# Key maxima spread one u product earlier, the subtractions on VectorE, and ten of sixteen channel weight rows split inside the second phase

## The chip, the cores and the metric

The kernel runs on one core of a Trainium2 chip. The metric is the device time of one execution in microseconds (us). The engines are named as in the profile: PE is TensorE, DVE is VectorE, ACT is ScalarE, POOL is GpSimd, and SP is the engine that issues most of the DMAs.

## What is computed

For each of 8 samples (576 tokens, 8 heads of 64) a linear attention feeds a gated block, and that feeds a channel block:

```
q_s = softmax(q, over head_dim); k_s = softmax(k, over the 576 tokens)
x   = q_s @ (k_s^T @ v)                       # 576 x 512 per sample
u, v = split(gelu(x @ w_in)); v_n = layernorm(v) * g_ln
x   = x + (u * (w_sg @ v_n + b_sg)) @ w_out
u   = x + token_mix(x; U, V)                  # rank 32
out = u + relu(u @ w_ch1) @ w_ch2             # 512 -> 2048 -> 512
```

The weights w_in, w_out, U, V, w_ch1 and w_ch2 are float64 in memory and are turned into pairs of float32 parts (a high and a low one) on the chip. A product of two such pairs is made with three matmuls: high by high, high by low, low by high.

## The kernel before

**Two phases.** The first phase loops over the samples, b = 0 to 7. In each it makes the v products (`emit_Vh`, tile pv, five token tiles t), the u products (`emit_Uh`, pu, four feature tiles f), the token products (`emit_S`, pS, four) and the output products (`emit_y`, py, four). The token mix of the sample before (`emit_yT`, `emit_U`, `emit_PV`; tiles pt, pp, pw) is woven into the v products, and the attention of the next sample into the rest. The second phase is the channel block: 9 blocks of 512 tokens, and in each 16 rows fc of channel weights. A step is `ch2` of one row (tile acc, 12 matmuls) and `ch1` of the row three further (tile ph, 12 matmuls). ACT writes the high part hh (L670), DVE the low part hl (L671).

**Who orders the work.** PE runs in program order throughout. In samples 1 to 6 DVE runs in program order too, and ACT, POOL and SP are ordered by the framework's planner. In sample 0, and from sample 7 to the end of the kernel, ACT runs in program order instead and DVE is ordered by the planner. PSUM products of the first phase share three buffers (`ps2`): a product has to wait until DVE or ACT has read the one three before it.

**The attention of the next sample.** `k_fold` takes the key maximum over token tiles, `k_max` transposes it on PE (pm), reduces it on DVE and builds two diagonal matrices on POOL; `k_spread` turns them into a broadcast on PE (pb), which ACT copies into kmx. `k_sub` subtracts it from five key tiles: tiles 0 and 1 on POOL, tiles 2 to 4 on DVE (all five on POOL for sample 1). `q_max` and `q_sub` do the same for queries per head, `q_total` sums the exponentials (DVE), `q_norm` multiplies by the reciprocal (all five on POOL).

**The pieces.** `Conv` converts one 128 x 256 piece of a float64 weight: a DMA brings the words into a buffer `stg`, a clamp (L163) makes the high word safe, ACT takes it to a float (L164), DVE shifts it (L170) and merges the low bits in (L171), ACT copies the high part and POOL subtracts to get the low part. `more(n)` takes n pieces one stage on; the tuples in `mid` and `spread` say how many are taken at each token tile t, each f and each output tile. A row of channel weights is four pieces. All 16 rows are converted in the first phase, with their clamp on DVE, and stored to `wd` in device memory; `load_w` reads them back through POOL's queue before the second phase uses them.

Of the kernel before, what the change touches and what calls it, by code (L numbers as in the profile page):

```python
# [8 lines left out]
F32 = mybir.dt.float32  # L9
F32R = mybir.dt.float32r  # L10
U32 = mybir.dt.uint32
# [11 lines left out]
def fused_kernel(tc, q, k, v, w_in, g_ln, w_sgT, b_sg, w_out, U, V, w_ch1, w_ch2, outT):  # L23
# [13 lines left out]
    LINE = 128  # L37
    VLEN = -(-(NT + 1) * NC * VW * 4 // LINE) * LINE // 4
    NFC = w_ch1.shape[0]
    BLK = 512  # L40
    NBLK = B * S // BLK
    TR = [P] * NT + [R]
# [6 lines left out]
    def tt(eng, out, a, b, op):  # L49
        return eng.tensor_tensor(out=out, in0=a, in1=b, op=op)  # L50
# [12 lines left out]
        return cm.__enter__(), lambda: cm.__exit__(None, None, None)  # L63

    dram, close_dram = opened("dram", space=bass.MemoryType.DRAM)
    wd = dram.tile([NFC, 2, P, 2, C], F32, name="wd")
    u2d = dram.tile([NC, P, B * S], F32, name="u2d")
    ps2, close_ps2 = opened("ps2", 3, space=PSUM)
    ps1, close_ps1 = opened("ps1", 2, space=PSUM)
# [18 lines left out]
    pool.memset(ones32, 1.0)  # L88
    ones = cst.tile([P, P], F32R, name="ones")
    pool.tensor_copy(ones, ones32)  # L90
    cpow = cst.tile([P, 2], F32, name="cpow")
    pool.memset(cpow[:, 0:1], 1e-6)
    pool.memset(cpow[:, 1:2], -0.5)

    qt = att.tile([P, NT + 1, C], F32, name="qt")
    gl = cst.tile([P, 24], F32, name="gl")[:, 0:NF]
# [44 lines left out]


    CW = 256

    def split_w(hi, lo, s, eng):
        copy(hi, s)
# [2 lines left out]
    def stage():  # L149
        return stgp.tile([P, S], F32, tag="stg", name="stg", bufs=5)  # L150

    def words(n):

        return stage().bitcast(U32)[:, 0 : 2 * n].rearrange("p (n j) -> p n j", j=2)

    def pairs(src):
        return src.bitcast(U32).rearrange("p (n j) -> p n j", j=2)

    def exponent(w, n, eng):

        t = stgp.tile([P, HS], F32, tag="f32", name="f32")[:, 0:n]
        hi = as_f32(w[:, :, 1])
        eng.tensor_scalar(out=hi, in0=hi, scalar1=F64_MOST, scalar2=-F64_MOST, op0=ALU.min, op1=ALU.max)  # L163
        act.activation(t, hi, AF.Prelu, scale=F64_SCALE, alpha=F64_SIGN)  # L164
        return t
# [109 lines left out]
            cols = slice(h * HS, (h + 1) * HS)  # L275
            yield ConvV(V[:, cols], lambda o=v_w[:, cols]: o, eng)

    def conv_ch(eng):

        for fc in range(NFC):  # L280
            for i, src in enumerate((w_ch1, w_ch2)):
                for c in range(0, C, CW):

                    def outs(fc=fc, i=i, cols=slice(c, c + CW)):
                        hl = stgp.tile([P, 2, CW], F32R, tag="chw", name="chw")
                        return hl[:, 0], hl[:, 1], lambda: sp.dma_start(wd[fc, i, :, :, cols], as_f32(hl))

                    piece = Conv(src[fc, :, c : c + CW], outs, eng)
                    piece.clamp = dve
                    yield piece  # L290
# [43 lines left out]
        km = kx_t[b] = tmpp.tile([P, S], F32, tag="gt", name="kmx")[:, 0:C]  # L334
        copy(km, pb.rearrange("p c e -> p (c e)"))

    def k_sub(b, t, eng=None):
        kt, n = k_t[b], TR[t]
        tt(eng if eng else pool if t < 2 or b == 1 else dve, kt[0:n, t], kt[0:n, t], kx_t[b][0:n], ALU.subtract)

    def k_exp(b):
        kt = k_t[b]
# [11 lines left out]
        dve.tensor_reduce(out=q_s[b][0 : TR[t], t], in_=q3(t), op=ALU.max, axis=mybir.AxisListType.X)  # L354

    def q_sub(b, t, eng=dve):
        eng = pool if b == 1 else eng
        n = TR[t]
        tt(eng, q3(t), q3(t), q_s[b][0:n, t].unsqueeze(2).to_broadcast([n, H, D]), ALU.subtract)

# [140 lines left out]
    def stats(b, t):  # L501
        ge, n = ln[b, t], TR[t]
        bst = tmpp.tile([P, 6], F32, tag="bst", name="bst", bufs=3)
        mv = tmpp.tile([P, 2], F32, tag="mv", name="mv", bufs=3)
        dve.bn_stats(out=bst[0:n], in_=ge[0:n])
        dve.bn_aggr(out=mv[0:n], in_=bst[0:n])
        tt(dve if b == 0 else pool, mv[0:n, 1:2], mv[0:n, 1:2], cpow[0:n, 0:1], ALU.add)
        last[pool] = tt(pool, mv[0:n, 1:2], mv[0:n, 1:2], cpow[0:n, 1:2], ALU.pow)
        ln[b, t] = (ge, mv)

    def emit_ln(b, t):
        ge, mv = ln.pop((b, t))
        n = TR[t]
        shift = tmpp.tile([P, 1], F32, tag="sh", name="sh", bufs=2)
        dve.scalar_tensor_tensor(
            out=shift[0:n], in0=mv[0:n, 0:1], scalar=-1.0, in1=mv[0:n, 1:2], op0=ALU.mult, op1=ALU.mult
        )
        act.activation(ge[0:n], ge[0:n], AF.Identity, bias=shift[0:n], scale=mv[0:n, 1:2])
        h = wrk.tile([P, F], F32R, tag=f"vh{t}", name=f"vh{t}")
        if t < NT:  # L520
            l = wrk.tile([P, F], F32R, tag=f"vl{t}", name=f"vl{t}")
            copy(h, ge)
            low(pool, l, ge, h)
            vh[b, t] = (h, l)
        else:
            copy(h[0:R], ge[0:R])
            low(dve, h[64 : 64 + R], ge[0:R], h[0:R])
            vh[b, t] = h
# [107 lines left out]
    def load_w(pl, fc):  # L636
        for i in range(2):
            hl = pl.tile([P, 2, C], F32R, tag=f"w{i}_{fc}", name=f"w{i}_{fc}", bufs=1)
            pool.dma_start(hl, wd[fc, i])
            w12[i, fc] = (hl[:, 0], hl[:, 1])  # L640

    blk = {}
# [77 lines left out]
            yield  # L720


    mid = ((0, 0, 0, 0, 0), (1, 1, 1, 1), (1, 1, 0, 0), (0, 1, 1, 1))
    spread = [mid] * B
    spread[0] = ((2, 2, 2, 2, 1), (2, 2, 2, 2), (1, 1, 1, 1), (1, 1, 1, 1))
    spread[B - 1] = ((0, 0, 0, 0, 1), (1, 1, 1, 1), (1, 1, 1, 0), (1, 1, 1, 1))
    order = {0: (act,), B - 1: (act,)}
    load_k(0)
    load_q(0)
    load_v(0)  # L730
# [8 lines left out]
    pieces.extend(conv_w_out(0, pool))  # L739
    pieces.extend(conv_w_out(CW, pool))  # L740
    pieces.extend(conv_uv(pool))
    pieces.extend(conv_ch(pool))
    with in_order(dve):
        run(k_fold(0))
        q_max(0, 0)
# [30 lines left out]
    for b in range(B):  # L776
# [11 lines left out]
        for t in range(NT + 1):  # L788
            emit_Vh(b, t)
            if nxt:  # L790
                if t == 0:
                    with behind(dve):
                        if b == 0:
                            q_max(nxt, 0)
                            q_max(nxt, 1)
                        q_max(nxt, 2)
                elif t == 1:
                    with behind(dve):
                        q_max(nxt, 3)
                        q_max(nxt, 4)  # L800
                elif t in (2, 3):
                    with behind(dve):
                        next(fold)
                        next(fold)
            if t < NT:
                stats(b, t)
            more(spread[b][0][t])
            if t > 0:
                emit_ln(b, t - 1)
            if t == NT:  # L810
                stats(b, t)
            if b > 0:
                for t2 in {0: (2,), 1: (3, 4)}.get(t, ()):
                    emit_yT(b - 1, t2)
            if t == 2 and b > 0:
                for t2 in range(NT + 1):
                    emit_U(b - 1, t2)
            if t in (3, 4) and b > 0:
                for c in range(2 * t - 6, 2 * t - 4):
                    emit_PV(b - 1, c)  # L820
# [1 line left out]
        if nxt:  # L822
            k_max(nxt)
        for f in range(NF):
            if nxt and f == 3:
                k_spread(nxt)
            if b == 0:
                more(spread[b][1][f])
            emit_Uh(b, f)
            if f == 0:  # L830
                emit_ln(b, NT)
                if nxt:
                    load_v(nxt)
            if nxt:
                with behind(pool):
                    if f == 0:
                        q_sub(nxt, 0)
                    elif f == 1:
                        q_sub(nxt, 1)
                        q_sub(nxt, 2)  # L840
                    elif f == 2:
                        q_sub(nxt, 3)
                        q_sub(nxt, 4)
                    elif f == 3:
                        for t in range(NT + 1):
                            k_sub(nxt, t)
            if b > 0:
                more(spread[b][1][f])
            if not nxt and f == 1:
                load_w(p2a, 0)  # L850
                split_u(p2a, 0)
        if nxt:
            for t in range(NT + 1):
                q_exp(nxt, t)
            k_exp(nxt)
            q_total(nxt)
            for t in range(NT + 1):
                q_norm(nxt, t)

        for f in range(NF):  # L860
            emit_S(b, f)
# [20 lines left out]
        for c in range(NC):  # L882
            more(spread[b][3][c])
            emit_y(b, c)
            if nxt and 0 < c < 3:
                emit_qT(nxt, 1 + c)
                if c == 2 and b + 2 < B:
                    load_q(b + 2)
        if b + 2 < B:
            q_max(b + 2, 0)  # L890
            q_max(b + 2, 1)
        if nxt:
            emit_xT(nxt, 0)
            emit_xT(nxt, 1)
# [27 lines left out]
    acc_p, close_acc = opened("acc_p", space=PSUM)  # L922
    p2w, close_p2w = opened("p2w", side="left")
    b_p, close_bp = opened("b_p", side="left")
    steps = [(n, fc) for n in range(NBLK) for fc in range(NFC)]
    for fc in range(3, NFC):
        load_w(p2w, fc)
    for i, (n, fc) in enumerate(steps):
        if fc == 2 and n + 1 < NBLK:
            load_u((p2a, b_p)[(n + 1) % 2], n + 1)  # L930
        if fc == 8 and n + 1 < NBLK:
            split_u((p2a, b_p)[(n + 1) % 2], n + 1)
        ch2(n, fc)
        if i + 3 < len(steps):
            n2, fc2 = steps[i + 3]
            ch1(n2, fc2, h_p.tile([P, BLK], F32, tag="ph", name="ph"), p2b)
    part.__exit__(None, None, None)
    for close in (close_bp, close_p2w, close_acc, close_hp, close_p2b, close_p2a, close_edge, close_dram):
        close()


# [38 lines left out]
```

## Time and profile before

| what | value |
|---|---|
| median of 3 runs | 1484.12 us (1480.53 to 1484.29) |
| profiled execution | 1485.02 us, span 1483.2 us |
| mean granted TensorE clock | 0.975 of full speed |
| PE busy | 1393.7 us, 94% of the span |
| DVE busy | 644.5 us, 43% |
| ACT busy | 481.4 us, 32% |
| POOL busy | 388.4 us, 26% |

Busy time counts each instruction from its start to its end. Matmuls overlap, so a busy PE is not one at its peak. An idle PE shows in the timeline as a bracket behind an instruction: how long PE had been idle before it, and whose work it was waiting for.

### The profile page before, as it was taken

Reading aid. Unit: us, or ns where it says so; the run is one execution under the profiler, and the core shown is the slowest. Engines: PE = TensorE matmul, PEld = TensorE weight load, DVE = VectorE, ACT = ScalarE, POOL = GpSimd, SP = SyncE. Lnnn points to the kernel's source line nnn. Section 1 sums busy time; section 2 is a strip of 40 time slices with the busy share of each in tenths; the row PEclk is TensorE's granted clock in tenths of the full one; section 3 lists DMA queues with packets and bytes.
Section 4 is the critical chain, followed back from the end, with each engine's and each line's share of the span. In section 5 each row is a group of like instructions: output and inputs, shape, how many; then the busy total and the mean of one; then the engine's idle time right before and its main releaser. Section 6 shows DMA issues by size and latency. Waiting matters only on the chain.

```text
span 1483.2 us, 19165 instructions
## 1 busy us (share of the span) xinstructions
PE 1393.7 (94%) x7672; PEld 1197.6 (81%) x7672; DVE 644.5 (43%) x1073; ACT 481.4 (32%) x842; POOL 388.4 (26%) x460
## 2 busy tenths in 40 slices
PE   4777989899989999999999999999999999999998
PEld 3666888888888888888888888888888888888887
DVE  7787777878777787755111111111111111111111
ACT  4554746465565656452011111111110111111110
POOL 6783443545353534541310101001010000101000
PEclk9998999999999999999999999999999999999999
DMA  6624234242524252343901010010101001010000
GB/s 175 186 78 133 87 123 121 87 149 85 154 95 146 97 160 83 111 142 107 370 0 57 1 57 1 20 38 0 57 1 57 0 8 50 0 57 1 29 0 29
DMA packets 80313, 117.01 MB, mean 79 GB/s; under 512 B 6496, under 2 KB 41312, under 8 KB 80224
## 3 DMA queue, kind: packets, MB, share of 16 engines
q1 hardware_dynamic: 75616, 99.02, 21.4%
q0 software_dynamic: 4608, 16.78, 3.3%
q8 instruction: 60, 0.98, 0.3%
q14 instruction: 29, 0.24, 0.0%
HBM read 80.12 MB, written 35.65 MB: 78 GB/s over the span
## 4 chain that ended last, share of the span: by engine, by line
PE 57%; DVE 1%; DMA 1%; issue 1%; ACT 0%; POOL 0%; DVEq 0%; ACTq 0%; SPq 0%; POOLq 0%
PE ph L47 26%; PE acc L47 26%; PE py L47 2%; PE pS L47 1%; PE pu L47 1%; PE pv L47 1%; DMA w<-wd 0%; DMA stg<-in_w_ch_dram 0%; PE pp L47 0%; DVE gl L50 0%; PE pt L594 0%; DVE gt L560 0%; DVE yl L50 0%; DVE xl L50 0%; POOL gt L50 0%
## 5 line engine op out<-in xcount | busy, mean ns | idle before, releaser
L47 PE MATMUL ph<-uh,w 128*128 128x512 f32 x1152 | 378.3, 389 | 0.1
L47 PE MATMUL acc<-hh,w 128*128 128x512 f32 x1152 | 377.7, 389 | 0.0
L671 DVE SCALAR_TENSOR_TENSOR hl<-ph,hh 128x512 fp32r<-128x512 f32 x144 | 99.5, 691 | 615.1 <-ACT hh L670 615.1
L670 ACT ACTIVATE hh<-ph 128x512 fp32r<-128x512 f32 x144 | 86.1, 598 | 685.2 <-PE ph L47 685.2
L47 PEld LDWEIGHTS acc<-hh,w 128*128 128x128 f32 x1152 | 216.4, 188 | 45.1
L47 PEld LDWEIGHTS ph<-uh,w 128*128 128x128 f32 x1152 | 216.1, 188 | 45.3 <-DMA w<-wd 0.5
L47 PE MATMUL ph<-ul,w 128*128 128x512 f32 x576 | 224.1, 389 | 0.0
L47 PE MATMUL acc<-hl,w 128*128 128x512 f32 x576 | 224.1, 389 | 0.0
L50 POOL TENSOR_TENSOR ul<-u,uh 128x512 fp32r<-128x512 f32 x32 | 40.3, 1295 | 590.5 <-ACT uh L56 590.5
L47 PEld LDWEIGHTS ph<-ul,w 128*128 128x128 f32 x576 | 108.2, 188 | 22.4
L47 PEld LDWEIGHTS acc<-hl,w 128*128 128x128 f32 x576 | 108.0, 188 | 22.2
L50 POOL TENSOR_TENSOR chw<-f,chw 128x256 fp32r<-128x256 f32 x64 | 55.7, 876 | 122.7 <-ACT chw L56 69.4
L47 PE MATMUL py<-gh,wo_h 128*128 128x288 f32 x256 | 63.2, 332 | 11.5 <-DVE gt L560 11.5
L47 PE MATMUL pS<-sg_h,vh 128*128 128x288 f32 x256 | 56.4, 302 | 15.2 <-DVE gt L560 9.3
L47 PE MATMUL pu<-xh,wi_h 128*128 128x288 f32 x256 | 58.9, 313 | 9.6 <-ACT ge L495 4.3
L47 PE MATMUL py<-gl,wo_h 128*128 128x288 f32 x256 | 60.3, 320 | 0.0
L47 PE MATMUL py<-gh,wo_l 128*128 128x288 f32 x256 | 59.4, 316 | 0.0
L47 PE MATMUL pu<-xl,wi_h 128*128 128x288 f32 x256 | 58.0, 310 | 0.0
L170 DVE TENSOR_SCALAR f<-f 128x256 uint32<-128x256 uint32 (+2 forms) x91 | 48.5, 533 | 21.7 <-ACT f L164 21.5
L47 PE MATMUL pu<-xh,wi_l 128*128 128x288 f32 x256 | 57.9, 309 | 0.0
L171 DVE SCALAR_TENSOR_TENSOR f<-stg,f 128x256 uint32<-128x256 uint32 (+2 forms) x91 | 56.0, 615 | 2.7
L47 PEld LDWEIGHTS py<-gh,wo_h 128*128 128x128 f32 x256 | 46.2, 213 | 13.5 <-issue 12.5
(146 smaller groups left out, 2282.6 us busy)
## 6 DMA issues: line engine op xcount, KB each, us to landing
stg<-in_w_ch_dram SPq DMA_DIRECT2D x64, 256.0 KB, 2.7
wd<-chw SPq DMA_DIRECT2D x64, 256.0 KB, 2.5
w<-wd POOLq DMA_DIRECT2D x32, 512.0 KB, 9.8
u2d<-yt SPq DMA_DIRECT2D x32, 288.0 KB, 2.1
u<-u2d SPq DMA_DIRECT2D x9, 1024.0 KB, 6.4
out_dram<-res SPq DMA_DIRECT2D x36, 256.0 KB, 2.1
vt<-in_v_dram SPq DMA_DIRECT2D x32, 256.0 KB, 6.9
qt<-in_q_dram SPq DMA_DIRECT2D x7, 1024.0 KB, 6.0
```

The costliest lines, as they stand in the source:

```text
L47: pe.matmul(out, lhsT, rhs, start=first, stop=last)
L50: return eng.tensor_tensor(out=out, in0=a, in1=b, op=op)
L170: dve.tensor_scalar(out=b, in0=b, scalar1=3, scalar2=None, op0=ALU.logical_shift_left)
L171: dve.scalar_tensor_tensor(out=b, in0=w[:, :, 0], scalar=29, in1=b, op0=ALU.logical_shift_right, op1=ALU.bitwise_or)
L670: act.activation(a, ph, AF.Relu)
L671: dve.scalar_tensor_tensor(out=l, in0=ph, scalar=0.0, in1=as_f32(a), op0=ALU.max, op1=ALU.subtract)
```

## The change

The edit has five parts. (1) Rows 0 to 5 of the channel weights are still converted in the first phase and go through device memory; rows 6 to 15 (40 pieces) are converted while the second phase runs, four pieces a step, straight into their weight tiles, with buffers of their own. Samples 1 to 6 now convert two pieces each, where they converted nine. (2) `k_spread` stands before the third u product instead of the fourth. (3) `k_sub` and `q_sub` run on DVE for every sample but sample 0's own queries, and the first two tiles of `q_norm` move from POOL to DVE. (4) The epsilon of the variance is added on DVE instead of POOL. (5) All five `q_max` of a sample stand at token tiles 0 to 2; sample 0 has DVE in program order and ACT ordered by the planner.

```diff
+    EARLY = 6
-    wd = dram.tile([NFC, 2, P, 2, C], F32, name="wd")
+    wd = dram.tile([EARLY, 2, P, 2, C], F32, name="wd")
...
-        return stage().bitcast(U32)[:, 0 : 2 * n].rearrange("p (n j) -> p n j", j=2)
+        if pools["stg"] is stgp:
+            s = stage()
+        else:
+            s = pools["stg"].tile([P, 2 * CW], F32, tag="stg", name="stg", bufs=4)
+        return s.bitcast(U32)[:, 0 : 2 * n].rearrange("p (n j) -> p n j", j=2)
...
                     def outs(fc=fc, i=i, cols=slice(c, c + CW)):
+                        if fc >= EARLY:
+                            h, l = w12[i, fc]
+                            return h[:, cols], l[:, cols]
...
-    def k_sub(b, t, eng=None):
+    def k_sub(b, t, eng=dve):
         kt, n = k_t[b], TR[t]
-        tt(eng if eng else pool if t < 2 or b == 1 else dve, kt[0:n, t], kt[0:n, t], kx_t[b][0:n], ALU.subtract)
+        tt(eng, kt[0:n, t], kt[0:n, t], kx_t[b][0:n], ALU.subtract)
...
     def q_sub(b, t, eng=dve):
-        eng = pool if b == 1 else eng
...
-        tt(dve if b == 0 else pool, mv[0:n, 1:2], mv[0:n, 1:2], cpow[0:n, 0:1], ALU.add)
-        last[pool] = tt(pool, mv[0:n, 1:2], mv[0:n, 1:2], cpow[0:n, 1:2], ALU.pow)
+        dve.tensor_scalar(out=mv[0:n, 1:2], in0=mv[0:n, 1:2], scalar1=1e-6, scalar2=None, op0=ALU.add)
+        tt(pool, mv[0:n, 1:2], mv[0:n, 1:2], half[0:n], ALU.pow)
...
-            pool.dma_start(hl, wd[fc, i])
+            if fc < EARLY:
+                pool.dma_start(hl, wd[fc, i])
...
-    mid = ((0, 0, 0, 0, 0), (1, 1, 1, 1), (1, 1, 0, 0), (0, 1, 1, 1))
+    mid = ((0, 0, 0, 0, 0), (0, 0, 0, 0), (0, 0, 0, 0), (0, 1, 1, 0))
-    spread[0] = ((2, 2, 2, 2, 1), (2, 2, 2, 2), (1, 1, 1, 1), (1, 1, 1, 1))
+    spread[0] = ((2, 2, 2, 1, 0), (2, 1, 1, 1), (3, 2, 2, 1), (1, 1, 1, 1))
-    order = {0: (act,), B - 1: (act,)}
+    order = {B - 1: (act,)}
...
-            if nxt and f == 3:
+            if nxt and f == 2:
                 k_spread(nxt)
...
+                for t in ((0, 1), (2, 3, 4), (), ())[f]:
+                    q_sub(nxt, t)
+                for t in ((), (), (0, 1), (2, 3, 4))[f]:
+                    k_sub(nxt, t)
...
-                q_norm(nxt, t)
+                q_norm(nxt, t, dve if t < 2 else pool)
...
+    pools["stg"], close_words = opened("words", side="left")
+    pieces.extend(conv_ch(range(EARLY, NFC), pool))
...
         ch2(n, fc)
+        more(4)
```

## Rows read from the trace of the kernel before

**Rows 1.** Windows: us, then busy PE, PEld, DVE, ACT, POOL, granted clock, DMA.

```profile
40.00:138.60 98.60, 73.05 (x480) 65.31 (x479) 76.33 (x120) 48.03 (x99) 63.80 (x76) 0.86 0.43 124
138.60:220.00 81.40, 75.38 (x528) 68.48 (x527) 61.92 (x107) 46.25 (x79) 36.34 (x42) 0.94 0.36 111
220.00:300.00 80.00, 73.45 (x535) 66.84 (x533) 61.86 (x107) 46.85 (x80) 36.19 (x42) 0.98 0.39 121
...
542.00:623.60 81.60, 75.84 (x532) 69.02 (x531) 63.11 (x112) 46.83 (x80) 36.42 (x42) 0.94 0.36 112
...
703.10:1483.20 780.10, 775.71 (x3422) 641.64 (x3420) 120.91 (x180) 100.95 (x173) 53.53 (x57) 1.00 0.12 40
```

**Rows 2.** Waits of PE over the span: total us, times, longest us.

```profile
PE py L47 <- DVE gt L560: 11.5, 7, 8.2
PE pt L429 <- DVE gt L560: 11.0, 6, 1.8
...
PE pS L47 <- DVE gt L560: 9.3, 6, 1.7
PE pw L47 <- DVE yt L50: 6.8, 7, 1.0
```

**Rows 3.** Windows of 10 us behind the pt wait, in two samples.

```profile
279.00:289.00 10.00, 7.64 (x45) 7.37 (x46) 9.57 (x19) 4.32 (x8) 2.78 (x3) 0.83 0.17 53
...
441.00:451.00 10.00, 7.91 (x37) 7.43 (x38) 9.40 (x18) 4.33 (x8) 2.77 (x3) 0.66 0.16 54
```

**Rows 4.** Timeline of DVE, 421 to 433 us: start, duration, instruction.

```profile
421.79 4.63 DVE L50 TENSOR_TENSOR kt<-kt,kmx 128x512 f32<-128x512 f32 x3
...
431.64 0.76 DVE L560 SCALAR_TENSOR_TENSOR gt<-pS,gl,bb 128x576 f32<-128x576 f32 x1
```

**Rows 5.** Timeline of POOL, 409 to 437 us.

```profile
409.68 1.04 POOL L50 TENSOR_TENSOR diag<-ident,ml 128x512 fp32r<-128x512 f32 x1
...
421.64 3.08 POOL L50 TENSOR_TENSOR kt<-kt,kmx 128x512 f32<-128x512 f32 x2 [4.25 <-ACT kmx L56]
...
431.54 5.33 POOL L50 TENSOR_TENSOR qt<-qt,qs 128x512 f32<-128x512 f32 x5 [0.50 <-DVE qs L370]
```

**Rows 6.** Timeline of PE, first and third u product of the same sample.

```profile
404.91 0.54 PE L47 MATMUL pu<-xh,wi_h 128*128 128x288 f32 x2 [0.42 <-DVE ge L50]
...
412.90 0.42 PE L47 MATMUL pu<-xh,wi_h 128*128 128x288 f32 x2
```

**Rows 7.** Timelines of DVE and PE in sample 0.

```profile
75.44 5.24 DVE L515 SCALAR_TENSOR_TENSOR sh<-mv 64x1 f32<-64x1 f32 x1 [0.72 <-POOL mv L50]
...
86.16 0.85 PE L47 MATMUL pS<-sg_h,vh 128*128 128x288 f32 x2 [5.84 <-ACT ut L540]
...
120.51 0.82 PE L47 MATMUL py<-gh,wo_h 128*128 128x288 f32 x2 [8.24 <-DVE gt L560]
```

**Rows 8.** Groups by line and form, whole span: count, busy us, mean ns.

```profile
L171 DVE SCALAR_TENSOR_TENSOR f<-stg,f 128x256 uint32<-128x256 uint32 x88 | 54.8, 622 | 2.7
L170 DVE TENSOR_SCALAR f<-f 128x256 uint32<-128x256 uint32 x88 | 46.6, 530 | 21.7 <-ACT f L164 21.5
```

**Rows 9.** Timelines of DVE and POOL, a piece with little beside it.

```profile
459.53 0.29 DVE L170 TENSOR_SCALAR f<-f 128x256 uint32<-128x256 uint32 x1
459.85 0.42 DVE L171 SCALAR_TENSOR_TENSOR f<-stg,f 128x256 uint32<-128x256 uint32 x1
...
460.86 0.74 POOL L50 TENSOR_TENSOR chw<-f,chw 128x256 fp32r<-128x256 f32 x1 [3.27 <-issue]
```

**Rows 10.** Second phase: timelines of ACT and DVE, and the chain that ended last.

```profile
656.90 2.18 ACT L56 ACTIVATE uh<-u 128x512 fp32r<-128x512 f32 x4
...
708.76 0.60 ACT L670 ACTIVATE hh<-ph 128x512 fp32r<-128x512 f32 x1 [7.17 <-PE ph L47]
...
715.25 0.69 DVE L671 SCALAR_TENSOR_TENSOR hl<-ph,hh 128x512 fp32r<-128x512 f32 x1 [5.17 <-ACT hh L670]
...
725.46 2.72 PE acc L47 x12
```

More of the change, by code (lines that the diff above doesn't have):

```diff
@@ L90, in fused_kernel @@
     pool.tensor_copy(ones, ones32)
-    cpow = cst.tile([P, 2], F32, name="cpow")
-    pool.memset(cpow[:, 0:1], 1e-6)
-    pool.memset(cpow[:, 1:2], -0.5)
+    half = cst.tile([P, 1], F32, name="half")
+    pool.memset(half, -0.5)
     qt = att.tile([P, NT + 1, C], F32, name="qt")
@@ L143, in fused_kernel @@
     CW = 256
+    pools = {"stg": stgp}
     def split_w(hi, lo, s, eng):
@@ L159, in exponent @@
     def exponent(w, n, eng):
-        t = stgp.tile([P, HS], F32, tag="f32", name="f32")[:, 0:n]
+        t = pools["stg"].tile([P, HS], F32, tag="f32", name="f32", bufs=3)[:, 0:n]
         hi = as_f32(w[:, :, 1])
@@ L276, in conv_uv, with conv_ch @@
             yield ConvV(V[:, cols], lambda o=v_w[:, cols]: o, eng)
-    def conv_ch(eng):
-        for fc in range(NFC):
+    def conv_ch(fcs, eng):
+        for fc in fcs:
             for i, src in enumerate((w_ch1, w_ch2)):
@@ L513, in emit_ln @@
         n = TR[t]
-        shift = tmpp.tile([P, 1], F32, tag="sh", name="sh", bufs=2)
+        shift = tmpp.tile([P, 1], F32, tag="sh", name="sh", bufs=4)
         dve.scalar_tensor_tensor(
@@ L741, in fused_kernel @@
     pieces.extend(conv_uv(pool))
-    pieces.extend(conv_ch(pool))
+    pieces.extend(conv_ch(range(EARLY), pool))
     with in_order(dve):
@@ L790, in fused_kernel @@
             if nxt:
[L791 to L802, printed above, removed]
+                with behind(dve):
+                    for t2 in ((0, 1), (2, 3), (4,), (), ())[t]:
+                        q_max(nxt, t2)
+                    if t in (2, 3):
                         next(fold)
@@ L834, in fused_kernel @@
             if nxt:
[L835 to L846, printed above, removed]
+                for t in ((0, 1), (2, 3, 4), (), ())[f]:
+                    q_sub(nxt, t)
+                for t in ((), (), (0, 1), (2, 3, 4))[f]:
+                    k_sub(nxt, t)
             if b > 0:
@@ L888, in fused_kernel @@
                     load_q(b + 2)
-        if b + 2 < B:
-            q_max(b + 2, 0)
-            q_max(b + 2, 1)
         if nxt:
@@ L937, in fused_kernel @@
     part.__exit__(None, None, None)
-    for close in (close_bp, close_p2w, close_acc, close_hp, close_p2b, close_p2a, close_edge, close_dram):
+    for close in (close_words, close_bp, close_p2w, close_acc, close_hp, close_p2b, close_p2a, close_edge, close_dram):
         close()
```

## Prediction

> **What bounds the kernel now.** I read the windows first, one per sample and one for the second phase. The second phase [rows 1] is 780.1 us with PE busy 775.7 at the full clock: nothing can be won there, only lost. The six middle samples run from 138.6 to 623.6 us, 485.0 us or 80.8 us each, with PE idle for some 6 us of each and a granted clock below one (0.94 in the first and the last of the six) [rows 1]. Sample 0 takes 98.6 us at 0.86, and DVE and POOL are busiest there: 76.3 and 63.8 us [rows 1]. So what can be won lies between 40 and 624 us, and there PE waits.
>
> The second view is the waits of PE. Three of them name the same work, DVE's read of a token product into gt: pS 9.3 us in 6 waits, pt 11.0 us in 6, and py 11.5 us in 7 [rows 2]. The longest of the py waits, 8.24 us, is sample 0's [rows 7], so the middle samples have 9.3 + 11.0 + (11.5 - 8.24) = 23.6 us, 3.9 us a sample. The pw wait (6.8 us in 7) [rows 2] is another kind: it comes in the v products.
>
> The third view is windows of 10 us just behind these waits. [...] PE had idled just before. [...] A sample pays 1.6 us (0.02 of 80.0) or 4.9 us (0.06 of 81.4) for the clock in all [rows 1]; I put the part behind the gt waits at 16 us over the six (four times 3.2, twice 1.6).
>
> The fourth view says why gt is late. DVE runs in program order, and before gt come the key subtractions (4.63 us for three, while POOL does two in 3.08 beside them), conversion instructions and q_total; gt starts at 431.64 [rows 4, 5]. Then POOL works off five q_norm in 5.33 us [rows 5] before it can multiply gt, and DVE's split waits for that.
>
> **The change, part by part.** *Conversions out of the middle samples.* Each loses seven pieces, six of them ahead of or among the gt reads. A piece is three DVE instructions; the clamp is priced like L170, a tensor_scalar of the same size. With little beside it that is 0.29 + 0.29 + 0.42 = 1.0 us [rows 9]; by the means of the span 0.53 + 0.53 + 0.62 = 1.7 us [rows 8]. Four pieces before gt(0) give DVE 4 to 7 us back, while PE's wait for it is about 1.5 us (9.3 over six) [rows 2].
>
> *Subtractions on DVE alone.* Five k_sub on DVE: 4.63 for three is 1.54 each while POOL holds its own two [rows 4, 5]. Alone I take the 0.69 us that another DVE subtraction of 512 columns takes [rows 10], so 5 x 0.69 = 3.5 us against 4.6; at worst, with 1.54 each, 7.7. Two q_norm come onto DVE ahead of gt: 2 x 0.69 = 1.4 us, at worst 3.1. The five epsilon additions are tiny; they shorten POOL's part of the variance and I take zero, hidden under DVE's waits for ACT. Together DVE reaches gt(0) earlier by 4 + 1.1 - 1.4 = 3.7 us, more than the 1.5 that was missing. At the worst prices for the moved and the best for the removed work it is 4 - 3.1 - 3.1 = -2.2, and the pS wait stays and grows.
>
> *POOL.* It keeps three q_norm, 3.2 us instead of 5.33, and starts them earlier by DVE's 3.7, so its gt product is free some 5.8 us earlier. The pt and py waits together are 14.3 us over six, 2.4 each [rows 2, 7]. They go too.
>
> *The broadcast one product earlier.* pb now stands where the third u product starts, 412.90 [rows 6], and needs the second diagonal, ready at 409.68 + 1.04 = 410.72 [rows 5]. That leaves 2.2 us here; in a sample without the low clock in these products (8.0 us from the first to the third here, less 1.7) it leaves about 0.5. Nothing lost; a slip of DVE by a microsecond would cost PE about 0.5 us a sample. If the cover goes, pb itself stalls PE, and the u products queue behind it. The earlier q_max adds two reductions to DVE's v products; they stand in places where it waits for ACT, so zero, and up to 1 us more at the pw wait.
>
> So the six samples get back 23.6 + 16 = 39.6 us at most. I keep 5 us for small new waits: **35 us**; bounds 15 (only the pt and py idle goes) and 46 (the clock behind pw as well).
>
> *Sample 0.* POOL did all ten subtractions of sample 1, and DVE stood behind it: a one-column instruction took 5.24 us [rows 7], and PE then waited 5.84 and 8.24 us [rows 7]. These 14.1 us should go, and with them some of the low clock: 0.14 of 98.6 is 13.8, which I halve because PE idles in part of it. That makes 21. Against it, DVE gets some 12 x 0.69 = 8 us of work and runs in program order, so a late weight DMA now blocks what stands behind it. I take **13 us**, bounds 0 and 25.
>
> *The second phase.* Forty pieces over ten steps, four to a step of 2 x 2.72 = 5.44 us [rows 10]. ACT runs in program order: four pieces' two ACT instructions stand before each step's hh, so a late piece delays hh. The first such group comes behind the hh that ends at 709.4, and the hh after it is needed by the acc at 725.46 [rows 10]. With T the time of four pieces and one hh and hl, nine groups in a row must fit: 9T + 2.2 (the block split that ACT does in the eighth step [rows 10]) has to stay under 725.46 + 8 x 5.44 - 1.3 (hh and hl) - 709.4 = 58.3 us, so T under 6.2. DVE needs 4 x 1.0 + 0.69 = 4.7 us a step with no one beside it [rows 9, 10] and 4 x 1.7 + 0.69 = 7.5 by the means [rows 8]. POOL's four subtractions are short here, 0.74 us [rows 9], where the means stem from times with POOL instructions over 1 us, so I take T nearer the lower, 5.8: it fits. At 7.5 the stall is 9 x 7.5 + 2.2 - 58.3 = 11.4 us. I charge **3 us** for scattered waits; bounds 0 and, with the clock falling behind the stalls, 25. The ten rows' way through device memory goes away and wins nothing, since PE barely waited for it.
>
> [...] The trace shows DVE and POOL in each other's way: DVE's three k_sub beside POOL's two took 1.54 us each [rows 4, 5]. [...]
>
> Sum: 35 + 13 - 3 = 45 us. The profiled execution took 1485.0 us (span 1483.2), 0.9 above the median of 1484.1, so the forecast is **1439 us** for the median.
>
> **The rivals.** *The second phase becomes bound by its pieces* (0.20). For it: DVE's means above, and ACT's fixed order, which lets one late DVE or DMA hold up hh. Against it: three steps of lead. T of 8 gives 9 x 8 + 2.2 - 58.3 = 16 us, and about 10 more for the clock: 1439 - 3 + 26 = 1462.
>
> *The gt waits move instead of going* (0.16). q_total can't start before ACT's exponentials, and DVE now does q_norm before gt. Then the six samples give 15, sample 0 gives 8: 1484 - 23 + 3 = 1464.
>
> *Everything goes, the pw clock too* (0.10): 46 + 20 - 0, 1418.
>
> [...]
>
> My forecast itself has 0.49, with 1427 to 1453 as its own range.
>
> **How the numbers follow.** 1439 is the likeliest case. The range 1420 to 1468 reaches to the first two rivals and nearly to the good one. About 0.3% (4.5 us) is what a measurement can tell from no change. Only the other side, and the ends of two rivals, come out over 1480: faster 0.91, same 0.03, slower 0.06.
>
> **What would show it.** Right: no PE wait for gt on pS, pt and py in the middle samples, each of them 73 to 76 us long; k_sub near 0.7 us each; sample 0 under 88 us; a step of the second phase at 5.44 us from the start. Wrong: a wait of PE on pb or kmx; acc waiting for DVE's hl or ph for a low weight part between 720 and 780 us; granted clock below one there; DVE in sample 0 waiting for a stg DMA.

## The result, and the profile after

The changed kernel takes 1440.34 us (median of 4 runs, 1439.39 to 1441.20) against 1482.56 for the kernel before on the same chip (4 runs): a ratio of 0.9716, 95% interval 0.9698 to 0.9733. The forecast was 1439. The profiled execution has a span of 1438.1 us, 45.1 less than before. The sum came out; its terms did not, and that their errors cancel is luck. Line numbers have moved by one to ten: `mm` is L48, the other helpers L51 and L57, clamp, Prelu, shift and merge of a piece L168, L169, L175 and L176, gt L567, hh and hl L678 and L679.

First the windows of after, with the columns of [rows 1], each sample from just before its first v product: sample 0, one of the six middle samples (five others read the same), sample 7 and its token mix, the steps with conversions, and the rest of the second phase.

```profile
40.00:129.30 89.30, 71.35 (x501) 64.97 (x500) 73.74 (x130) 56.42 (x107) 52.27 (x64) 0.90 0.46 139
129.30:201.20 71.90, 71.06 (x529) 65.09 (x529) 51.23 (x96) 42.04 (x65) 25.74 (x27) 1.00 0.28 82
...
560.70:643.40 82.70, 77.17 (x465) 68.17 (x464) 47.92 (x91) 35.85 (x70) 27.76 (x33) 0.98 0.45 149
643.40:720.00 76.60, 66.96 (x276) 51.87 (x275) 53.68 (x126) 34.31 (x89) 37.08 (x47) 0.97 0.54 173
720.00:1438.10 718.10, 714.25 (x3148) 591.01 (x3146) 114.29 (x171) 93.98 (x162) 36.99 (x31) 1.00 0.07 24
```

The windows of [rows 1] begin a sample some 2.5 us earlier, among the products ahead of its v products. Cut at the same place as in after, the kernel before has for sample 0, samples 1 to 6 together and sample 7:

```profile
40.00:141.00 101.00, 75.45 (x500) 67.71 (x499) 76.94 (x122) 50.44 (x104) 65.38 (x78) 0.86 0.43 127
141.00:625.70 484.70, 448.03 (x3164) 407.48 (x3164) 372.72 (x649) 278.50 (x469) 217.91 (x253) 0.95 0.38 116
625.70:703.10 77.40, 74.32 (x465) 66.25 (x465) 44.24 (x74) 33.13 (x62) 25.66 (x35) 1.00 0.39 126
```

Stage by stage:

| stage | before | after | change | predicted |
|---|---|---|---|---|
| sample 0 | 101.0 | 89.3 | -11.7 | -13 |
| samples 1 to 6 | 484.7 | 431.4 | -53.3 | -35 |
| sample 7 | 77.4 | 82.7 | +5.3 | 0 |
| second phase | 780.1 | 794.7 | +14.6 | +3 |

The middle samples won 18.3 us more than forecast, and the second phase lost 11.6 more, sample 7 5.3 more, and sample 0 won 1.3 less: 18.3 - 18.2.

The second view is the waits of PE over the span, as in [rows 2].

```profile
PE pm L320 <- DVE km L51: 16.7, 2, 8.7
...
PE py L48 <- DVE gt L567: 5.7, 2, 5.5
PE acc L48 <- DVE hl L679: 5.4, 7, 1.5
PE acc L48 <- ACT hh L678: 4.3, 2, 4.0
...
PE pt L436 <- DVE gt L567: 1.7, 1, 1.7
...
PE pw L48 <- DVE yt L51: 0.6, 1, 0.6
```

The gt waits of the six samples are gone: the one pt wait and the py wait of 5.5 us are sample 0's. So is the pw wait of each sample, which the forecast had left in place. In return there are a pm wait (7.97 us in sample 0; the other one lies before it) and two kinds of wait on acc, 9.7 us together, where before the second phase had next to none. A middle sample has 71.90 us with PE busy for 71.06 at the full clock, so by these rows some 0.8 us is left there.

Third, the timeline of DVE in a middle sample, the columns as in [rows 4].

```profile
375.65 3.08 DVE L51 TENSOR_TENSOR kt<-kt,kmx 128x512 f32<-128x512 f32 x5
...
383.53 0.80 DVE L567 SCALAR_TENSOR_TENSOR gt<-pS,gl,bb 128x576 f32<-128x576 f32 x1
385.98 0.82 DVE L567 SCALAR_TENSOR_TENSOR gt<-pS,gl,bb 128x576 f32<-128x576 f32 x1 [1.65 <-PE pS L48]
```

The five key subtractions take 3.08 us, 0.62 each, where three had taken 4.63 beside POOL's two [rows 4, 5]; and ahead of the second gt DVE waits 1.65 us for PE. The order of who waits for whom has turned round.

### The profile page after: what moved, and what is told of

Its sections match the earlier page's. It is cut to its first block, busy times and chain, and to the rows that moved or that the text cites. A ratio compares the mean times of both kernels' runs of the same rounds, so it can differ in the third digit from the quotient of the medians.

```text
span 1438.1 us, 18961 instructions
## 1 busy us (share of the span) xinstructions
PE 1376.5 (96%) x7672; PEld 1181.2 (82%) x7672; DVE 627.7 (44%) x1144; ACT 491.0 (34%) x846; POOL 335.0 (23%) x368
## 4 chain that ended last, share of the span: by engine, by line
PE 80%; DVE 7%; DMA 5%; ACT 4%; issue 2%; POOL 1%; SPq 0%; ACTq 0%; POOLq 0%; DVEq 0%
PE acc L48 25%; PE ph L48 25%; PE py L48 8%; PE pS L48 6%; PE pu L48 5%; PE pv L48 4%; DMA stg<-in_w_ch_dram 4%; PE pk L48 1%; PE pt L436 1%; DVE f L175 1%; DVE f L176 1%; ACT xh L57 1%; PE pp L48 1%; ACT x L57 1%; DVE yt L51 1%
## 5 line engine op out<-in xcount | busy, mean ns | idle before, releaser
L48 PE MATMUL acc<-hh,w 128*128 128x512 f32 x1152 | 379.9, 391 | 4.3 <-ACT hh L678 4.3
L48 PE MATMUL ph<-uh,w 128*128 128x512 f32 x1152 | 378.2, 389 | 0.0
L679 DVE SCALAR_TENSOR_TENSOR hl<-ph,hh 128x512 fp32r<-128x512 f32 x144 | 99.4, 690 | 560.4 <-ACT hh L678 560.3
L678 ACT ACTIVATE hh<-ph 128x512 fp32r<-128x512 f32 x144 | 85.9, 597 | 626.0 <-PE ph L48 626.0
L48 PEld LDWEIGHTS acc<-hh,w 128*128 128x128 f32 x1152 | 217.3, 189 | 49.9 <-ACT hh L678 5.1
L48 PEld LDWEIGHTS ph<-uh,w 128*128 128x128 f32 x1152 | 216.4, 188 | 45.0
L48 PE MATMUL acc<-hl,w 128*128 128x512 f32 x576 | 226.1, 393 | 5.4 <-DVE hl L679 5.4
L48 PE MATMUL ph<-ul,w 128*128 128x512 f32 x576 | 224.1, 389 | 0.0
L51 POOL TENSOR_TENSOR ul<-u,uh 128x512 fp32r<-128x512 f32 x32 | 40.6, 1304 | 560.5 <-ACT uh L57 560.5
L48 PEld LDWEIGHTS acc<-hl,w 128*128 128x128 f32 x576 | 108.7, 189 | 31.5 <-DVE hl L679 9.0
L48 PEld LDWEIGHTS ph<-ul,w 128*128 128x128 f32 x576 | 108.2, 188 | 22.4
L48 PE MATMUL py<-gh,wo_h 128*128 128x288 f32 x256 | 58.9, 312 | 6.7 <-DVE gt L567 5.7
L48 PE MATMUL py<-gl,wo_h 128*128 128x288 f32 x256 | 56.8, 304 | 1.5 <-DVE gl L51 1.5
L48 PE MATMUL pu<-xh,wi_h 128*128 128x288 f32 x256 | 56.3, 301 | 0.6 <-DVE yt L51 0.6
L48 PE MATMUL py<-gh,wo_l 128*128 128x288 f32 x256 | 56.5, 302 | 0.0
L48 PE MATMUL pS<-sg_l,vh 128*128 128x288 f32 x256 | 55.0, 296 | 0.5 <-DVE sg_l L51 0.5
L48 PE MATMUL pS<-sg_h,vh 128*128 128x288 f32 x256 | 55.0, 296 | 0.5 <-ACT ut L547 0.5
L48 PE MATMUL pu<-xl,wi_h 128*128 128x288 f32 x256 | 55.4, 298 | 0.0
L48 PE MATMUL pu<-xh,wi_l 128*128 128x288 f32 x256 | 55.2, 297 | 0.0
L48 PE MATMUL pS<-sg_h,vl 128*128 128x288 f32 x256 | 55.0, 295 | 0.0
L48 PE MATMUL pv<-wi_h,xl 128*128 128x512 f32 x128 | 51.6, 403 | 3.4 <-DVE xl L51 3.4
L51 POOL TENSOR_TENSOR vl<-ge,vh 128x512 fp32r<-128x512 f32 x32 | 44.6, 1395 | 40.3 <-ACT vh L57 40.3
```

Source lines behind the costliest of these rows:

```text
L48: pe.matmul(out, lhsT, rhs, start=first, stop=last)
L678: act.activation(a, ph, AF.Relu)
L679: dve.scalar_tensor_tensor(out=l, in0=ph, scalar=0.0, in1=as_f32(a), op0=ALU.max, op1=ALU.subtract)
```

## The experiments

All ratios are to the kernel before, run on the same chip. The first five runs take the change apart; the others go after what the windows left open.

**The rows back in the first phase, the rest of the change kept.**

```diff
-    EARLY = 6
+    EARLY = 16
-    mid = ((0, 0, 0, 0, 0), (0, 0, 0, 0), (0, 0, 0, 0), (0, 1, 1, 0))
+    mid = ((0, 0, 0, 0, 0), (1, 1, 1, 1), (1, 1, 0, 0), (0, 1, 1, 1))
```

> All sixteen rows are converted in the first phase again (nine pieces a middle sample, as before); every other edit of the change stays. My theory (taking the conversions off VectorE is what clears the waits for gt): most of them stay, a middle sample takes 78 to 80 us, sample 0 about 89 as in the changed kernel, the second phase 780, together 1460 to 1472 us. The rival (the subtractions on VectorE alone and the quieter POOL clear them): a middle sample at 72 to 74 us, and since the second phase loses nothing, 1425 to 1435 us, faster than the changed kernel.

1460.37 us, ratio 0.9852 (0.9832 to 0.9872). First the window of one sample, then the waits of PE:

```profile
210.60:288.90 78.30, 73.70 (x528) 67.45 (x528) 63.03 (x117) 46.44 (x79) 32.17 (x33) 0.96 0.40 121
```

```profile
PE pS L48 <- DVE gt L567: 23.4, 6, 4.5
```

The wait for the first gt is left and has grown, from 9.3 to 23.4 us over the six samples, 3.9 each, with the low clock behind it; the pt, py, pu and pw waits of these samples are gone. From the first v product of sample 1 to that of sample 7 the attention edits alone take 14.4 us out (484.7 to 470.3).

**The rows moved, the rest as before.** The kernel before with the row edits of the diff: EARLY, the `words` buffers, `conv_ch(range(EARLY, NFC), pool)` and `more(4)` in the second phase, and the new `mid`.

> The kernel before with only the ten rows moved into the second phase; subtractions, broadcast, q_norm, epsilon, q_max and the order of sample 0 stay as they were. My theory: a middle sample at 74 to 76 us without a wait for gt, sample 0 at 96 to 98, the second phase 795, together 1453 to 1465 us. The rival (the attention edits do it): a middle sample at 78 to 80 us, together 1475 to 1495 us.

1470.09 us, ratio 0.9917 (0.9894 to 0.9941). Window of one sample and waits of PE:

```profile
219.20:294.50 75.30, 71.86 (x524) 65.64 (x524) 49.77 (x85) 41.74 (x65) 30.47 (x35) 0.98 0.26 77
```

```profile
PE py L48 <- DVE gt L569: 12.7, 7, 8.3
...
PE pw L48 <- DVE yt L51: 6.7, 7, 1.0
...
PE pu L48 <- DVE ge L51: 4.2, 7, 1.6
```

The rows alone take 32.3 us out of the six samples (484.7 to 452.4). Their pS and pt waits for gt are gone; the pw and pu waits stay, with their clock, and so does the wait for gt at py: 12.7 - 8.3 = 4.4 us over the six, where it was 3.3. Sample 0 is as long as before, and the whole is 5 us over the range expected. 14.4 and 32.3 make 46.7, and together the parts give 53.3: the last 6.6 us come only with both. Each alone leaves a wait for gt.

**What in the attention edits removes the pw and pu waits.** Three runs undo one edit each in the kernel after. The broadcast and the subtractions back before the fourth product:

```diff
-            if nxt and f == 2:
+            if nxt and f == 3:
                 k_spread(nxt)
...
-                for t in ((), (), (0, 1), (2, 3, 4))[f]:
+                for t in ((), (), (), (0, 1, 2, 3, 4))[f]:
                     k_sub(nxt, t)
```

> The changed kernel with the broadcast before the fourth u product again, and all five key subtractions behind it. My theory: VectorE has room before the third token product now, so a middle sample stays at 72 us, together 1439 to 1442 us. The rival (the earlier broadcast is what brings gt in time): gt's first read comes some 3 us later, PE waits 1 to 2 us for it in six samples and falls to the low clock behind it, 1448 to 1458 us.

1440.45 us, ratio 0.9713 (0.9697 to 0.9729), and a middle sample still takes 71.9 us: the broadcast's place is worth nothing. Two key subtractions and all five normalizations back on POOL:

```diff
-                    k_sub(nxt, t)
+                    k_sub(nxt, t, pool if t < 2 else dve)
...
-                q_norm(nxt, t, dve if t < 2 else pool)
+                q_norm(nxt, t)
```

> The changed kernel with two key subtractions and all five q_norm on POOL as before. My theory: with the conversions gone there is slack, a middle sample 72 to 73 us, together 1440 to 1446 us. The rival (subtracting on VectorE alone carries the gain): waits of pt and py for gt of 1 to 2 us and the low clock behind them, a middle sample 75 us or more, together 1455 to 1465 us.

1442.66 us, ratio 0.9730 (0.9715 to 0.9744); the six samples take 434.2 us, 0.5 each more on the mean. The epsilon back on POOL:

```diff
-        dve.tensor_scalar(out=mv[0:n, 1:2], in0=mv[0:n, 1:2], scalar1=1e-6, scalar2=None, op0=ALU.add)
+        tt(dve if b == 0 else pool, mv[0:n, 1:2], mv[0:n, 1:2], eps[0:n], ALU.add)
```

> Only the epsilon addition goes back to POOL (sample 0 keeps it on DVE), so that POOL again does two one-column instructions behind every variance. If this short chain is what kept the v products' buffers and so made PE wait at pw before the change, the middle samples grow from 71.9 to 73 to 74.3 us, with a pw wait of about 1 us in each, and the whole is 1447 to 1455 us. If the pw wait went because of the maxima and key folds, which stand in other places now, the middle samples stay at 71.9 us and the whole at 1440 us.

1442.33 us, ratio 0.9732 (0.9717 to 0.9746). PE's timeline, the first v product of two samples in a row, and PE's waits between them:

```profile
201.37 0.40 PE L48 MATMUL pv<-wi_h,xh 128*128 128x512 f32 x1
...
273.82 0.40 PE L48 MATMUL pv<-wi_h,xh 128*128 128x512 f32 x1
```

```profile
PE pu L48 <- DVE ge L51: 0.4, 1, 0.4
```

72.45 us a sample, 0.55 more, and it is the pu wait that comes back, not pw. So my expectation of a pw wait was wrong. Of the 3.5 us a sample between the rows alone (75.4) and the whole change (71.9), these three account for 0.0, 0.5 and 0.55. Some 2.5 us are left by elimination, and no run says for what. The kernels still differ there in the places of the query maxima and query subtractions and in the order hints around them, and the buffer of sh has four copies instead of two; none of these was run alone. The key folds of these samples stand at the same token tiles in both kernels, so they are not it.

**Where the second phase loses its 14.6 us.** The timeline of after, ACT, DVE and PE, shows three things:

```profile
620.23 0.28 DVE L168 TENSOR_SCALAR stg<-stg 128x256 f32<-128x256 f32 x1
...
646.00 0.42 ACT L169 ACTIVATE f<-stg 128x256 f32<-128x256 f32 x1
...
655.96 0.29 DVE L168 TENSOR_SCALAR stg<-stg 128x256 f32<-128x256 f32 x1 [9.98 <-DMA stg<-in_w_ch_dram]
656.17 0.28 DVE L175 TENSOR_SCALAR f<-f 128x256 uint32<-128x256 uint32 x1
656.49 0.43 DVE L176 SCALAR_TENSOR_TENSOR f<-stg,f 128x256 uint32<-128x256 uint32 x1
656.95 0.42 ACT L57 ACTIVATE w<-f 128x256 fp32r<-128x256 f32 x1 [9.20 <-DVE f L176]
657.27 0.58 ACT L678 ACTIVATE hh<-ph 128x512 fp32r<-128x512 f32 x1
665.74 0.58 ACT L678 ACTIVATE hh<-ph 128x512 fp32r<-128x512 f32 x1
...
689.52 0.58 ACT L678 ACTIVATE hh<-ph 128x512 fp32r<-128x512 f32 x1
...
702.73 0.58 ACT L678 ACTIVATE hh<-ph 128x512 fp32r<-128x512 f32 x1
703.21 2.18 ACT L57 ACTIVATE uh<-u 128x512 fp32r<-128x512 f32 x4
...
706.15 0.50 PE L48 MATMUL acc<-hl,w 128*128 128x512 f32 x1 [1.53 <-DVE hl L679]
...
715.67 0.80 PE L48 MATMUL acc<-hh,w 128*128 128x512 f32 x1 [4.01 <-ACT hh L678]
```

The start: in the first step four pieces are begun and three finished ahead of the hh. Their words were there: DVE had clamped the last of the four by 620.5 us. The third piece's Prelu on ACT is done at 646.42, but DVE, which the planner orders here, takes the fifth piece's clamp next and stands 9.98 us at it for words. Only then come the third piece's shift (656.17) and merge (656.49), ACT makes the copy for which it stood 9.20 us, and the hh behind it comes at 657.27. In [rows 10] the same hh came 5.66 us behind the first acc, which here would be 649.1: 8.2 us of the lead are gone. The DMA view of 640 to 660 us (KB each, median us from issue to landing) names what the fifth piece's words waited beside:

```profile
w<-wd POOLq DMA_DIRECT2D x5, 512.0 KB, 8.9
stg<-in_w_ch_dram SPq DMA_DIRECT2D x3, 256.0 KB, 10.1
```

The step: from 665.74 to 689.52 the hh are (689.52 - 665.74) / 4 = 5.95 us apart, then come steps of 7.20 and 6.01 us, and the first had taken 8.47. From 657.27 to 702.73 that is 6.49 us each over seven, where PE needs 5.44. And the block split of 2.18 us stands in ACT's order among the last pieces. Six runs tested these.

Seven rows early, and no pieces in the first step:

```diff
-    EARLY = 6
+    EARLY = 7
+    spread[1] = spread[2] = ((0, 0, 0, 0, 0), (0, 0, 0, 0), (0, 0, 0, 0), (0, 1, 1, 1))
...
-        more(4)
+        more(4 if i else 0)
```

> Seven rows in the first phase instead of six, and the second phase takes its four pieces a step from its second step on, so that the first step, where the words' DMAs queue behind the weight loads, has none. If the late start costs the second phase its lead: first waits of acc gone, only the one at the block split left, 1428 to 1433 us. If the rate does it (6.07 us for four pieces and a step, against 5.44): waits of acc from the third or fourth piece step on as in the changed kernel, 1437 to 1441 us.

1435.83 us, ratio 0.9689 (0.9668 to 0.9711). The hh behind the first acc now come at 651.20 and 658.26 us, and one hl wait of 0.6 us is left of seven. The two samples with a third piece still take 71.8 and 71.9 us. The wait on hh at the split stays (4.25 us). So the late start did cost the lead. The gain fell short of the expected one: sample 7, which has more of the early pieces, takes 85.3 us, 2.6 more than in after, and the seven steps from 651.20 to 699.13 take 6.85 us each.

Three pieces a step instead of four:

```diff
-        more(4)
+        more(3)
```

> Three pieces a step in the second phase instead of four, over fourteen steps. If the rate does it: a step needs some 4.7 us for its pieces, hh is never late after the start, 1427 to 1431 us, with at most the wait at the block split left. If the late start does it: the first steps still wait some 1 to 3 us and the low clock behind them stays, 1435 to 1439 us.

1442.22 us, ratio 0.9730 (0.9707 to 0.9753). A miss for both sides: with a quarter fewer pieces the hh are 6.02 us apart again from 671.27 to 689.33. Up to there PE hardly waits; from 691 us on it waits for weights (ph on ACT's w, 7.8 us in 5 waits up to 725 us), since the pieces come later. So the length of these steps is not DVE's work alone: from 660 to 690 us it stands 6.3 us, in 12 waits, at clamps without words.

The first block split four steps later:

```diff
-        if fc == 8 and n + 1 < NBLK:
+        if fc == (8 if n else 12) and n + 1 < NBLK:
```

> The changed kernel with the second block's split moved from the eighth to the twelfth row of the first block, behind the last piece. If ACT's four copies and POOL's 5.3 us of subtractions in the middle of the pieces make the last wait of acc (4.0 us) and the low clock behind it: that wait goes, 1432 to 1436 us. If it is only the last instalment of a rate that is too low: the wait appears anyway, spread over the steps, 1438 to 1441 us.

1436.06 us, ratio 0.9679 (0.9658 to 0.9700). The wait of 4.0 us is gone; eight hl waits of 5.7 us together stay.

Five word buffers instead of four (and three output buffers instead of four):

```diff
-            s = pools["stg"].tile([P, 2 * CW], F32, tag="stg", name="stg", bufs=4)
+            s = pools["stg"].tile([P, 2 * CW], F32, tag="stg", name="stg", bufs=5)
```

> Five word buffers instead of four in the second phase (paid for with three result buffers instead of four). If a step's 6.07 us are the round trip of a word buffer (DMA, clamp, ACT, merge, next DMA), which holds four pieces: a step falls to 5.4 us, the waits of acc on hl go but for the first one and the one at the split, 1432 to 1437 us. [...]

1441.46 us, ratio 0.9721 (0.9704 to 0.9738). The steps are 5.8 to 7.4 us. Not the round trip of the buffers.

Three pieces under way at a time (with six word and five float buffers for them, and the output's buffers opened behind the last piece):

```diff
-            if len(begun) > 1 or (begun and not loaded and not pieces):
+            if len(begun) > depth[0] or (begun and not loaded and not pieces):
...
+    depth[0] = 2
```

> In the second phase three pieces are under way at a time instead of two (six weight buffers, five for the pieces; the output's buffers are opened behind the last piece), so that ACT does the Prelu of a piece two pieces ahead of the copy. If the 6.05 us are the way of two pieces through ACT and DVE, the steps fall to 5.44 us, at which PE sets them, the hl waits between 660 and 700 us go, and the whole is 1431 to 1437 us. If DVE's order or its instructions' length beside POOL set them, the steps stay at 5.9 us or more, and the whole is 1438 to 1443 us.

1436.30 us, ratio 0.9690 (0.9676 to 0.9705). Steps of 6.4 to 6.8 us behind the first two and hl waits of 9.0 us together: the way of a piece through ACT and DVE does not set the step either. It is 4 us faster all the same, with no wait on hh at the split; the granted clock from 700 to 735 us is 0.95 instead of 0.90, which is 1.8 us of it, and the rest was not traced. Window of 660 to 700 us in after, and in this run:

```profile
660.00:700.00 40.00, 35.90 (x150) 27.52 (x150) 34.90 (x84) 21.39 (x56) 19.73 (x25) 1.00 0.52 164
```

```profile
660.00:700.00 40.00, 36.20 (x153) 28.34 (x154) 35.11 (x85) 20.37 (x55) 19.09 (x24) 1.00 0.50 158
```

In both DVE is busy for 87% of the window, ACT and POOL for about half.

DVE in program order in the second phase:

```diff
+    part.__exit__(None, None, None)
+    part = in_order(act, dve)
+    part.__enter__()
     for i, (n, fc) in enumerate(steps):
```

> In the second phase DVE runs in program order, as ACT does, and no longer in the planner's. If the 6.05 us between two hh come from DVE's order (a clamp that waits for its weights ahead of a shift or merge that could run), the steps fall to at most 5.6 us, the hl waits of PE between 660 and 700 us go, and the whole is 1433 to 1437 us. If they come from the way through ACT and DVE with only two pieces under way at a time, the steps stay at 6.0 us or grow, and the whole is 1439 to 1446 us.

1432.19 us, ratio 0.9666 (0.9648 to 0.9685). The time that the order theory gave; its way holds at the start, not for the step. The timeline of ACT, DVE and POOL, first the start and then one step:

```profile
648.92 0.60 ACT L678 ACTIVATE hh<-ph 128x512 fp32r<-128x512 f32 x1 [1.03 <-PE ph L48]
...
676.32 1.63 POOL L51 TENSOR_TENSOR w<-f,w 128x256 fp32r<-128x256 f32 x2 [1.14 <-ACT w L57]
677.01 0.58 ACT L678 ACTIVATE hh<-ph 128x512 fp32r<-128x512 f32 x1
677.62 0.69 DVE L679 SCALAR_TENSOR_TENSOR hl<-ph,hh 128x512 fp32r<-128x512 f32 x1 [0.97 <-ACT hh L678]
...
679.30 0.29 DVE L175 TENSOR_SCALAR f<-f 128x256 uint32<-128x256 uint32 x1
...
679.71 1.69 POOL L51 TENSOR_TENSOR w<-f,w 128x256 fp32r<-128x256 f32 x2 [1.76 <-ACT w L57]
679.96 0.83 DVE L168 TENSOR_SCALAR stg<-stg 128x256 f32<-128x256 f32 x1
...
680.72 0.82 DVE L175 TENSOR_SCALAR f<-f 128x256 uint32<-128x256 uint32 x1
...
683.23 0.58 ACT L678 ACTIVATE hh<-ph 128x512 fp32r<-128x512 f32 x1
```

The first hh comes at 648.92, where [rows 10] put it, 8.4 us earlier than in after, and no acc waits for hl until the split. The fifth piece's clamp stands behind hl now (650.16), and no shift or merge that this hh's copies need stands behind a clamp without words. Later words are late all the same: a clamp waits 2.98 us for them, until 654.96, and the second hh comes 9.45 us behind the first. The six steps after that are 6.21 or 6.22 us each (here 677.01 to 683.23), no shorter than before. So the gain is lead, not pace. The pace can be read here: DVE waits 0.97 us for hh, and its instructions beside POOL's two take 0.83 and 0.82 us instead of the 0.29 that they take alone, 1.1 us a step. Without the wait and these two the step would be some 4.1 us of DVE. In after, where the planner orders DVE, the idle times fall elsewhere; why it comes to 6 us and more there is not settled.

**Together, with sample 0's folds earlier.** DVE's program order, the late split, a third piece in the middle samples' y products and six fewer in sample 7; and in sample 0 the key folds one token tile earlier, ahead of the query maxima:

```diff
-    mid = ((0, 0, 0, 0, 0), (0, 0, 0, 0), (0, 0, 0, 0), (0, 1, 1, 0))
+    mid = ((0, 0, 0, 0, 0), (0, 0, 0, 0), (0, 0, 0, 0), (0, 1, 1, 1))
-    spread[B - 1] = ((0, 0, 0, 0, 1), (1, 1, 1, 1), (1, 1, 1, 0), (1, 1, 1, 1))
+    spread[B - 1] = ((0, 0, 0, 0, 1), (1, 1, 1, 0), (0, 0, 0, 0), (0, 0, 1, 1))
...
-                    for t2 in ((0, 1), (2, 3), (4,), (), ())[t]:
+                    for t2 in (((0, 1), (2, 3), (4,), (), ()) if b else ((), (), (), (0, 1, 2), (3, 4)))[t]:
...
-                    if t in (2, 3):
+                    if t in ((2, 3) if b else (1, 2)):
```

> Four edits together, each of which shows in windows of its own: in sample 0 the key folds of sample 1 stand one token tile earlier and the query maxima behind them; samples 1 to 6 take a third piece at the y products and the last sample six fewer; DVE runs the second phase in program order; the first block split stands in the thirteenth step. If PE's 7.97 us at pm come from the folds' place behind the conversions, that wait falls to 3 us or less; sample 0 gains 3 to 5 us if PE's order was the limit there, and nothing (the wait comes back at gt) if DVE's work is. With six fewer pieces the last sample loses its py waits and the low clock behind them, 3 us, unless these come from elsewhere. In the second phase the last wait on hh and its low clock go, 4 to 5 us against 1432.2. By the theory that each of these waits has its own cause the whole is 1418 to 1426 us; by the rival, that a wait removed comes back at the next place, it stays at 1428 to 1432 us.

1421.57 us, ratio 0.9601 (0.9580 to 0.9623), 18.8 us under the kernel after (17 by the two ratios). Windows of a middle sample, sample 7 and the second phase:

```profile
128.60:200.50 71.90, 71.08 (x530) 65.10 (x529) 52.16 (x99) 42.98 (x67) 26.55 (x28) 1.00 0.29 87
560.50:638.70 78.20, 74.74 (x466) 66.80 (x466) 42.11 (x79) 32.87 (x61) 21.86 (x27) 1.00 0.38 129
638.70:1419.80 781.10, 776.18 (x3421) 641.34 (x3419) 161.25 (x292) 129.91 (x248) 75.47 (x77) 1.00 0.11 38
```

The second phase now takes 781.1 us, 1.0 more than before the change, with all ten rows converted in it; sample 7 takes 4.5 us less than in after; the middle samples carry the third piece for nothing. Sample 0 is where the rival was right. Timeline of PE and DVE:

```profile
55.56 0.66 PE L320 MATMUL pm<-ident,km 128*128 128x128 f32 x4 [0.82 <-DVE km L51]
...
70.00 0.67 DVE L322 TENSOR_REDUCE mx<-pm 128x4 f32<-128x512 f32 x1
...
73.19 0.79 PE L48 MATMUL pb<-diag,ones 128*128 128x512 f32 x1 [6.95 <-POOL diag L51]
```

The pm wait falls from 7.97 to 0.82 us, and PE stands 6.95 us at pb instead: the reduction of pm runs on DVE only at 70.00, in program order behind the query maxima and the last tile's variance. From its first v product to the next sample's, sample 0 takes 88.8 us, within the 88.3 to 90.0 of the seven kernels here that have sample 0 as in after: no gain that can be told.

## Why the forecast held, and which steps failed

**The middle samples: the mechanism was right, the size 18.3 us too small.** Conversions out, DVE earlier at gt, POOL free earlier, the three gt waits gone: all as argued. The rows alone clear pS and pt, the attention edits alone pt and py, and only both clear all three. The subtractions took 0.62 us each where I said 0.7. What failed is the step that left the pw wait and the clock behind it in place, and said that the earlier query maxima would cost "up to 1 us more at the pw wait". The pw and pu waits went instead, and with them all of the low clock. The bound "46 (the clock behind pw as well)" was too low too: 484.7 / 6 - 71.9 = 8.9 us a sample is everything that a sample lost to idle PE and clock. The number to read was PE's busy time less what the low clock adds to it: 73.5 - 1.6 and 75.4 - 4.9, some 70.5 to 71.9 us [rows 1]. What lies above that was all to be had, as my third rival said for these samples. The second, waits that move instead of going, came true in sample 0 alone. The forecast for a sample, 73 to 76 us, was missed on the good side. No run shows the 16 us for the clock behind the gt waits as a term of its own: the 10 us of [rows 3] had 0.83 and 0.66, and over the six samples the clock went from 0.95 to 1.00 and PE's busy time from 448.03 to 426.38 us, for 3164 matmuls recorded in both.

**The broadcast.** Its margin held, and it is worth nothing either way. The epsilon, costed at zero, is worth 0.55 us a sample through the pu wait.

**Sample 0: 13 forecast, 11.7 measured, inside the bounds.** The pS wait of 5.84 us went, and the py wait fell from 8.24 to 5.46. The warning that DVE in program order lets late work block what stands behind it came true, at pm: the key folds stand behind a shift that waits for ACT. The last run moved the folds, and the wait came back further on; DVE is busy for 73.7 of the 89.3 us. What bounds sample 0 now stays open.

**Sample 7** was costed at nothing, and lost 5.3 us. DVE stands 8.1 us at clamps without words there, where it stood 1.5 before, PE waits 2.7 us at py, where it did not wait, and the clock is 0.98 where it was 1.00. Four of the second phase's 40 clamps fall here too, since 36 come after 645 us. Six pieces fewer gave 4.5 us back.

**The second phase: 3 us forecast, 14.6 measured; the first rival in part.** The sum had T at 5.8 us, and under 6.2 it was to fit. Two of its numbers failed. One is its start: it let the first group begin behind an hh that comes on time, but the first step's pieces stand ahead of that hh, and it was 8.2 us late. The other is T: 6.49 us over the seven steps to 702.73, and 9 x 6.49 + 2.2 + 8.2 - 58.3 = 10.5 us of stall follow. The waits on acc are 9.7 us, and the low clock behind the last one (0.90 of the 35 us from 700) adds 3.5; the last 1.4 us were not traced. The form of the sum came near: with the start on time, T of 6.85 (seven rows early) gives 5.5 us, and PE waited 0.6 + 4.25; 6.68 from 648.92 to 695.65 (DVE in program order) gives 4.0, and PE waited 3.7. The rival had named this way: ACT's fixed order, in which one late DVE holds up hh. What made DVE late was the order that the planner gave it. I had named the DMA's delay as a sign, but only for sample 0. With lead restored and the split moved, the same pieces cost 1.0 us. The other side, which had 0.05 of the chances, was a low clock through all ten steps. It did not come: the granted clock is 1.00 from 657.27 to 715 us, with PE busy for 84% of it, and 0.97 over the whole window of the steps with conversions.

**DVE beside POOL.** In the run with DVE in program order a clamp and a shift beside POOL take 0.83 and 0.82 us instead of 0.29, while hl takes 0.69 us at 677.62 beside POOL's 676.32, and 0.68 to 0.69 throughout after. Why hl is not longer there was not shown. In the step shown two of DVE's thirteen instructions paid, 1.1 us. Measured steps of 6.2 us in this order, and of 6.49 on the mean in after's, lie between my 5.8 and the 7.5 by the means.

## What to carry to other kernels

Bound what a stage can win by the busy time of its bound engine at the full clock, not by the waits that the change is aimed at: here, once those went, small ones and their clock went too (71.06 of 71.90 us busy, at 1.00). When work moves to a stage with slack, price its first round apart from its rate: here the first round's lead is 8.2 of the 10.5 us in the sum above. And ask of every engine, whoever orders it, what its first blocked instruction holds up: a shift behind a clamp without words on DVE, and through it ACT's hh behind a copy; PE's u products behind pm.

## What was not expected of the hardware

Loads of 256 KB on SP's queue landed 10.1 us after their issue (median of three) while five loads of 512 KB ran on POOL's queue and four stores of 288 KB had gone ahead on SP's; their median over the span is 2.7 us. And PE showed no loss from the other engines' work beside it: in the run with DVE in program order, the window of 660 to 700 us has DVE busy for 83% of it, and PE for all of it at the full clock.

```profile
660.00:700.00 40.00, 40.00 (x178) 33.13 (x177) 33.31 (x80) 24.55 (x59) 23.14 (x27) 1.00 0.52 159
```
